# Two PSUM banks as tiles of their own, y's transposes in one earlier list, unused rows filled by DMA, and sums moved within the step

## The chip, the core and the metric

The kernel runs on one core of a Trainium2 chip. The core has a matrix engine (TensorE, PE in the profile, whose weight loads stand apart as PEld), VectorE (DVE), ScalarE (ACT), GpSimd (POOL) and SyncE (SP), which here issues every DMA. Each engine works through its own list of instructions in order and waits on semaphores for the others. The metric is the device time of one execution in microseconds (us), lower is better.

## The reference

`x` has 8 sequences of 4160 rows and 192 columns. First a causal convolution over 7 rows, with one softmax-normalised set of taps for each of 8 heads of 24 columns. Its output, 33280 rows of 192, goes through a small network: 192 to 1024, a SoLU (the hidden value times its softmax), a layer norm with a gain, and 1024 back to 192. Everything is float32.

```python
def _attn_ref(x, weight):
    w = np.exp(weight - weight.max(-1, keepdims=True))
    w = w / (w.sum(-1, keepdims=True) + 1e-09)
    x_pad = np.concatenate([np.zeros((B, K - 1, D)), x], axis=1)
    out = np.einsum('hk,bskhg->bshg', w, x_unf)     # x_unf: 7 shifted views of x_pad
...
def _moe_ref(x, w_in, w_out, g_ln):
    h = x @ w_in
    e = np.exp(h - h.max(-1, keepdims=True))
    solu = h * (e / (e.sum(-1, keepdims=True) + 1e-09))
    mu, var = solu.mean(-1, keepdims=True), solu.var(-1, keepdims=True)
    return ((solu - mu) / np.sqrt(var + 1e-06) * g_ln) @ w_out
```

## The kernel before

**Tiles, chunks, steps.** The 33280 rows are 260 tiles of 128 rows. The convolution works on chunks: chunks 0 to 2 (class `Chunk`, 8, 8 and 16 tiles) and chunks 3 to 16 (class `Strips`, 16 tiles, the last two 18). A chunk's convolution is done while the chunk before it goes through the network. From tile 8 on the network runs in steps of three tiles a, b, c (`three_steps`). As 16 is not a multiple of 3, a chunk's first tile is the first, second or third tile of a step in turn: chunk 3 first, 4 second, 5 third, and so on; chunk 2 third, 15 and 16 first.

**One tile's way.** PE multiplies y (float16 in a high and a low part) with w_in (`emit_rows` L799, `emit_third` L822) into a pair of PSUM banks. There are three pairs, for a, b and c of each step. DVE takes the maximum (`emit_max` L853), ACT the exponential (`emit_exp` L860), DVE the product (`emit_mul` L870), which is the last reader of the pair. ACT writes its high half (`emit_hi` L878), POOL the low one (`emit_lo` L890), a DMA transposes both (L892, on SP's list), and five tiles later PE multiplies them with w_out (`emit_out` L922) into a single PSUM bank. DVE evacuates it (`emit_evac` L932); POOL scales the rows (L1001); SP stores them (L1014).

**The single banks.** Of PSUM's eight banks six are the pairs. The last two are one tile, `both`, of 1024 columns. `single()` gives its halves in turn: one to each output product, and both to each group of a strip convolution. A group (`Strips.product` L385, `nc.tensor.matmul` L399) covers two heads, half of the chunk's tiles in each bank. One copy over both banks on ACT (`upper` L280) gives the high part of y in `y16`, one on DVE (`lower` L289) the low part. Heads 4 and 5 straddle a block of y16, so this group is copied in two pieces: five copies a chunk on each engine.

**y's transposes.** `y16` has three blocks of 128 columns: block 0 the high part of columns 0 to 127, block 2 their low part, block 1 both parts of the rest. Each is transposed by DMA (`turn` L419) into `yT`, in two halves of the chunk's tiles: six transposes a chunk. One copy (`double` L427) then brings part of yT's block 1 into `y2`, for the low products of L822. y16 is single, yT and y2 are double.

**The order.** `chores` says at which of its chunk's tiles k a piece of work for later chunks is due; a step takes those of its three tiles. A step's transposes are appended to the list `moves` at its end. `move()` takes one of them after each tile's p transpose: after a's, after b's, and at the end. The copy `double` is issued in the next step, after b. A step begins with the loads (`load` L356); two loads of the chunk after the next two are due at k = 13 and 14, the others at k = 1 and 3. Where a sequence begins within a chunk, POOL clears 16 rows behind the load (L365). The sums over a chunk's rows (`sum_squares` L377, DVE, "peak" in `chores`) scale y; they are due at k = 1, 4, 7 and 10 (6, 7, 9 and 10 in chunk 2, whose loads are due at k = 4 and 6) and stand near the step's end, between the maximum and the product of c. In a strip tile the partitions 48 to 63 and 112 to 127 hold nothing; `clear` (L442) sets the whole tile to zero once, on POOL, four times in all.

## Time and profile before

| | |
|---|---|
| time, median of 3 runs | 1426.57 us (1426.14 to 1429.6) |
| the profiled execution's time | 1433.29 us |
| its span, first to last instruction | 1431.6 us |
| busy: PE, DVE, ACT, POOL | 1175.8, 987.7, 950.3, 768.6 us |
| DMA queue's share of 16 engines' span | 91.8% |
| granted TensorE clock, mean | 0.935 |

The profile is of one execution. The rows below name an instruction by engine and line (PE ... L922 is line 922), with what it writes and reads (`both<-ohl,pT`). SPq is SP's list of DMA issues; the time of such a row is that of the issue, not of the transfer. Times in a timeline count from the span's start. "[0.76 <-DVE raw L932]" says that the engine was idle for 0.76 us before the row, and which instruction ended the wait.

### The profile page before, as it was taken

The numbers are of one execution on the slowest core, as the hardware profiler recorded it, in microseconds if no ns is written. First come the engines' busy times: TensorE is split into PE (matmuls) and PEld (weight loads), VectorE is DVE, ScalarE is ACT, GpSimd is POOL, SyncE is SP. The second block draws the span as 40 slices with busy tenths as digits, with TensorE's granted clock in tenths as the row PEclk, the third lists the DMA queues.
The fourth block names the chain that finished last, engine by engine and source line by source line (L and its number), as shares of the span: only waits on it lengthen the run. The fifth ranks groups of instructions, "written<-read, shape, count | busy, mean of one in ns | idle before, by whom it ended". The sixth has DMA issues, their size and how long they took to land.

```text
span 1431.6 us, 23903 instructions
## 1 busy us (share of the span) xinstructions
PE 1175.8 (82%) x8854; PEld 667.4 (47%) x8854; DVE 987.7 (69%) x1666; ACT 950.3 (66%) x1543; POOL 768.6 (54%) x751
## 2 busy tenths in 40 slices
PE   5877786979779698896969979598896969989997
PEld 3654443545445354453535545354453535545555
DVE  7755585768658586684857768377684847867777
ACT  6854565767647576584757757477674847777785
POOL 2635453646545455563654745357355536656674
PEclk8989898999989899898989989799898989999999
DMA  7696799999889989988999898799989899988977
GB/s 205 120 153 115 127 185 160 161 182 166 152 151 181 178 151 164 187 156 153 181 170 167 160 185 156 145 169 171 169 164 174 160 177 160 177 153 152 193 146 159
DMA packets 733747, 233.91 MB, mean 163 GB/s; under 512 B 649102, under 2 KB 732222, under 8 KB 733630
## 3 DMA queue, kind: packets, MB, share of 16 engines
q1 hardware_dynamic: 733630, 232.38, 91.8%
q8 instruction: 69, 1.13, 0.3%
q14 instruction: 48, 0.39, 0.1%
HBM read 40.50 MB, written 25.56 MB: 46 GB/s over the span
## 4 chain that ended last, share of the span: by engine, by line
PE 33%; DVE 19%; POOL 15%; issue 12%; ACT 8%; DMA 8%; SPq 4%; DVEq 0%; POOLq 0%; ACTq 0%
PE both L922 15%; PE ph L799 13%; POOL p L890 10%; DVE ph L853 8%; DVE e L870 7%; ACT e L860 4%; DMA xs<-in_x_dram 3%; ACT y L280 3%; PE both L399 3%; SPq L892 3%; DMA yT<-y 2%; DVE raw L932 2%; POOL raw L1001 2%; DMA pT<-p 2%; PE ph L822 1%
## 5 line engine op out<-in xcount | busy, mean ns | idle before, releaser
L890 POOL TENSOR_TENSOR p<-e,p 128x1024 f16<-128x1024 f32 x257 | 547.1, 2137 | 523.3 <-ACT p L878 523.1
L922 PE MATMUL both<-ohl,pT 128*128 128x192 f16 (+1 forms) x4264 | 568.4, 288 | 103.2 <-DVE raw L932 71.0
L922 PEld LDWEIGHTS <-pT 128*128 128x128 f16 x4264 | 394.6, 100 | 291.5 <-issue 136.5
L799 PE MATMUL ph<-whi,yT 128*128 128x512 f16 x1548 | 433.4, 390 | 78.5 <-DMA yT<-y 74.6
L860 ACT ACTIVATE e<-ph,sm 128x1024 f32<-128x1024 f32 x260 | 289.6, 1114 | 233.9 <-DVE ph L853 218.7
L853 DVE TENSOR_SCALAR_CACHE_REDUCE ph<-ph,cv 128x1024 f32<-128x1024 f32 x259 | 329.5, 1288 | 135.0 <-PE ph L799 100.1
L870 DVE SCALAR_TENSOR_TENSOR e<-ph,cv,e 128x1024 f32<-128x1024 f32 x259 | 331.0, 1278 | 28.3 <-ACT e L860 22.1
L799 PEld LDWEIGHTS <-yT 128*128 128x128 f16 x2064 | 194.7, 100 | 322.2 <-DMA yT<-y 79.0
L878 ACT CAST p<-e 128x1024 f16<-128x1024 f32 x257 | 267.0, 1039 | 83.0 <-DVE e L870 81.7
L882 ACT ACTIVATE sq<-e 128x1024 f32<-128x1024 f32 x260 | 273.4, 1051 | 0.2
L289 DVE SCALAR_TENSOR_TENSOR y<-both,s,y 128x768 f16<-128x768 f32 (+10 forms) x85 | 66.8, 805 | 212.8 <-ACT y L280 175.9
L799 PE MATMUL ph<-wlo,yT 128*128 128x512 f16 x516 | 156.3, 385 | 0.0
L932 DVE TENSOR_REDUCE raw<-both 128x192 f32<-128x384 f32 x247 | 136.7, 554 | 26.9 <-PE both L922 20.4
L280 ACT ACTIVATE y<-both,s 128x768 f16<-128x768 f32 (+10 forms) x85 | 60.1, 731 | 134.7 <-PE both L399 112.0
L822 PE MATMUL ph<-wlo,y 64*128 64x512 f16 x251 | 71.6, 390 | 49.8 <-DMA y<-yT 49.8
L1001 POOL TENSOR_SCALAR raw<-raw,t 128x192 f32<-128x192 f32 x240 | 99.8, 429 | 0.0
L822 PE MATMUL ph<-wlo,yT 64*128 64x512 f16 x269 | 75.4, 386 | 0.0
L993 POOL TENSOR_TENSOR t<-t,mhalf 128x8 f32<-128x8 f32 (+2 forms) x33 | 53.6, 1623 | 2.6
L377 DVE TENSOR_REDUCE xa<-xr 128x1 f32<-128x1536 f32 (+1 forms) x28 | 49.5, 1771 | 3.4 <-DMA xr<-in_x_dram 3.4
L860 ACT ACTIVATION_READ_ACCUMULATOR e<-ph,sm 128x1 f32 x260 | 50.1, 193 | 0.0
L377 DVE TENSOR_REDUCE xa<-xs 128x1 f32<-128x1536 f32 (+1 forms) x28 | 49.4, 1771 | 0.0
L882 ACT ACTIVATION_READ_ACCUMULATOR sq<-e 128x1 f32 x260 | 49.2, 189 | 0.0
(143 smaller groups left out, 452.9 us busy)
## 6 DMA issues: line engine op xcount, KB each, us to landing
out_dram<-raw SPq DMA_DIRECT2D x127, 192.0 KB, 2.9
xs<-in_x_dram SPq DMA_DIRECT2D x24, 576.0 KB, 7.7
xr<-in_x_dram SPq DMA_DIRECT2D x24, 576.0 KB, 7.9
pT<-p SPq DMA_TRANSPOSE x263, 4.5
y<-yT SPq DMA_DIRECT2D x12, 256.0 KB, 3.7
xr<-in_x_dram SPq DMA_DIRECT2D x6, 480.0 KB, 5.9
xs<-in_x_dram SPq DMA_DIRECT2D x4, 648.0 KB, 8.0
xr<-in_x_dram SPq DMA_DIRECT2D x4, 648.0 KB, 8.3
```

The costliest lines, as they stand in the source:

```text
L280: act.activation(self.at(0, col + e, col + z, a, b), pc[:, :, e:z], AF.Copy, scale=self.scale(),)
L799: nc.tensor.matmul(bank, lhs, w[:, r, n * 512 : (n + 1) * 512], start=start and j == 0, stop=stop and j == len(ops) - 1,)
L822: nc.tensor.matmul(banks_of(t)[n], y[q, t.off : t.off + P], wlo[q, 1, n * 512 : (n + 1) * 512], start=start, stop=not start,)
L853: dve.tensor_scalar(t.ph, t.ph, t.cv[:, 0:1], None, ALU.mult, ALU.min, accum_out=t.bias)
L860: act.activation(t.e, t.ph, AF.Exp, bias=t.bias, scale=-1.0, accum_out=grp.z[:, g : g + 1])
L870: dve.scalar_tensor_tensor(t.e, t.ph, t.cv[:, 3:4], t.e, ALU.mult, ALU.mult, accum_out=t.grp.s1[:, t.g : t.g + 1],)
L878: act.copy(t.p16[:, :, 0, :], t.halves)
L882: act.activation(junk, t.e, AF.Square, accum_out=t.grp.s2[:, t.g : t.g + 1])
L890: eng.tensor_tensor(t.p16[:, :, 1, :], t.halves, t.p16[:, :, 0, :], ALU.subtract)
L922: nc.tensor.matmul(t.po[:, 0:n], t.pT[:, a, :], w, start=j == 0, stop=j == len(ops) - 1)
L932: dve.tensor_reduce(t.grp.raw[:, t.g, :], t.po[:, 0 : 2 * D].rearrange("p (a d) -> p d a", a=2), AX.X, ALU.add,)
L1001: pool.tensor_scalar(o, o, u, 1.0, ALU.mult, ALU.mult)
```

## The change

- The two single banks become tiles of their own, `single0` and `single1`. A strip convolution takes one of each, and `upper` and `lower` copy each by itself: ten copies a chunk on each engine instead of five.
- `double` becomes an entry of the list of transposes (block 3). The list's due tiles go from 5, 5, 10, 10, 10, 10 (and 8 for the copy) to 4, 4, 7, 9, 9, 12, 12, one later in chunk 2. Chunk 2's own last transposes are all due at its first tile.
- The unused rows are filled by two DMAs from a tile of zeros, in place of a memset of the whole strip tile; the four calls move.
- From tile 16 on the sums stand at the beginning of the step's DVE work, ahead of `lower` and a's maximum.

```diff
@@ -90,14 +90,12 @@
         return ps.tile([P, F], F32, name=name, tag=f"pair{slot}")
 
     singles = 0
-    both = ps.tile([P, F], F32, name="both")
 
     def single(name):
 
         nonlocal singles
         singles += 1
-        k = singles % 2 * 512
-        return both[:, k : k + 512]
+        return ps.tile([P, 512], F32, name=name, tag=f"single{singles % 2}")
 
 
     def total(parts, name, bank=None):
@@ -384,12 +382,13 @@
 
         def product(self, h, n, a, z, bank=None):
 
-            single(f"pc_{self.ch}_{h}a"), single(f"pc_{self.ch}_{h}b")
-            self.bank = both[:, 512:F]
             m = self.nt // 2
-            pc = both[:, 512 - m * n * HD : 512 + m * n * HD].rearrange(
-                "p (t e) -> p t e", e=n * HD
-            )
+            banks = [single(f"pc_{self.ch}_{h}_{late}") for late in range(2)]
+            self.bank = banks[1]
+            pc = [
+                t[:, 0 : m * n * HD].rearrange("p (t e) -> p t e", e=n * HD)
+                for t in banks
+            ]
             for j in range(n):
                 for half, c in STRIPS:
                     late, own = (half + c) % 2, slice(64 * half, 64 * half + ROWS)
@@ -397,10 +396,7 @@
                         "p (t g) d -> p g t d", g=2
                     )
                     nc.tensor.matmul(
-                        pc[
-                            Q * c : Q * (c + 1), late * m : (late + 1) * m,
-                            j * HD : (j + 1) * HD,
-                        ],
+                        pc[late][Q * c : Q * (c + 1), :, j * HD : (j + 1) * HD],
                         taps[own, h + j, 64 * half : 64 * half + Q],
                         raw[:, c // 2, :, (h + j) * HD : (h + j + 1) * HD],
                         start=j == 0, stop=j == n - 1,
@@ -410,12 +406,24 @@
         def scale(self):
             return self.s
 
+        def upper(self, pc, h, n, a, b):
+            m = self.nt // 2
+            for late in range(2):
+                super().upper(pc[late], h, n, late * m, (late + 1) * m)
+
+        def lower(self, pc, h, n, a, b):
+            m = self.nt // 2
+            for late in range(2):
+                super().lower(pc[late], h, n, late * m, (late + 1) * m)
+
         def at(self, low, col, z, a, b):
 
             blk, c = divmod(col + low * (2 * P if col < P else R), P)
             return y16[:, blk, a:b, c : c + z - col]
 
         def turn(self, blk, a, z):
+            if blk == NB:
+                return self.double(a, z)
             nc.sync.dma_start_transpose(
                 self.yT[:, blk, a * P : z * P].rearrange("p (w t) -> p w t", t=P),
                 y16[:, blk, a:z, :].rearrange("p w d -> p (w d)"),
@@ -438,8 +446,12 @@
             )
 
     def clear(k, late):
-        a, z = (0, NTM)
-        pool.memset(strips[k][late][:, a:z, :], 0.0)
+
+        for half in range(2):
+            nc.sync.dma_start(
+                strips[k][late][64 * half + ROWS : 64 * (half + 1)],
+                zero.unsqueeze(1).broadcast_to([64 - ROWS, NTM, D]),
+            )
 
     chunks = [(Chunk if ch < OLD else Strips)(ch) for ch in range(NCH)]
 
@@ -476,6 +488,8 @@
     rebias = cp.tile([P, 1], F32, name="rebias")
     pool.memset(rebias, -916.0 * 2.0**23)
     act.activation(rebias[0:1], rebias[0:1], AF.Copy)
+    zero = cp.tile([64 - ROWS, D], F32, name="zero")
+    pool.memset(zero, 0.0)
     mhalf = cp.tile([P, 1], F32, name="mhalf")
     pool.memset(mhalf, -0.5)
     band = cp.tile([TJ, H, TB, K], F32, name="band")
@@ -1078,19 +1092,18 @@
         else:
             late = ch == 2
             if late:
-                turn(c0, c0.parts[1], 0.01, 0.2)
-                fixed("clear", (1, 4), ((1, 0), (1, 1)))
+                turn(c0, c0.parts[1], 0.001, 0.002)
+                fixed("clear", (1,), ((1, 1),))
             if c1:
                 m = c1.nt // 2
                 fixed("conv", [q + late for q in (0, 3, 6, 9)], [(c1, hg) for hg in c1.groups()])
                 fixed("open", [4], [c1])
-                fixed("turn", [5 + late] * 2 + [10 + late] * 4, [
+                fixed("turn", [q + late for q in (4, 4, 7, 9, 9, 12, 12)], [
                     (c1, q) for q in (
-                        (1, 0, m), (1, m, 2 * m), (0, 0, m), (2, 0, m),
+                        (1, 0, m), (1, m, 2 * m), (3, 0, 2 * m), (0, 0, m), (2, 0, m),
                         (0, m, 2 * m), (2, m, 2 * m),
                     )
                 ])
-                fixed("double", [8 + late], [(c1, (0, 2 * m))])
             if c2:
                 fixed("load", (4, 4, 6, 6) if late else (-1, -1, 1, 3), [(c2, j) for j in range(4)])
                 fixed("peak", (6, 7, 9, 10) if late else (1, 4, 7, 10),
@@ -1101,6 +1114,7 @@
             sums(c2, 0.75, 1.0)
             put(0.5, 0.875, "load", [(c3, j) for j in range(4)])
         if ch == 1:
+            fixed("clear", (3,), ((1, 0),))
             fixed("peak", (0, 1, 3, 4), [(c2, h) for j in range(4) for h in c2.halves(j)])
         return got
 
@@ -1254,7 +1268,6 @@
             emit_lo(q, pool)
         out_root()
         first_strips()
-        clear(0, 0)
 
     def third_two(i):
 
@@ -1287,6 +1300,7 @@
         for q in (tiles[3], t):
             emit_square(q)
         early.clear()
+        clear(0, 0)
         clear(0, 1)
         for q in (t, u):
             work = chores(q.ch, q.k, q.n)
@@ -1448,7 +1462,8 @@
                     sum_up(k, h, i - 1)
         if not start:
             root_squares()
-        if not start:
+            for k, h in work.get("peak", []):
+                sum_up(k, h, i + 2)
             lowers(0)
             emit_max(a)
         else:
@@ -1515,8 +1530,9 @@
             emit_evac(d)
         lowers(3)
         run_rows(i)
-        for k, h in work.get("peak", []):
-            sum_up(k, h, i + 2)
+        if start:
+            for k, h in work.get("peak", []):
+                sum_up(k, h, i + 2)
         run_rows(i)
         numerators(c)
         if at(3):
```

## The prediction, made before the changed kernel was run

> **What bounds the kernel now.** I read the page first (busy shares, queues), then the list of waits, then the timeline of one ordinary step, then the ends of three chunks, then the forms of the copies.

> ```profile
> span 1431.6 us, 23903 instructions
> ...
> PE 1175.8 (82%) x8854; PEld 667.4 (47%) x8854; DVE 987.7 (69%) x1666; ACT 950.3 (66%) x1543; POOL 768.6 (54%) x751
> ...
> q1 hardware_dynamic: 733630, 232.38, 91.8%
> ```

> No engine is full; PE is the busiest, and the DMA engines show 91.8%. So the list of waits (who, for whom: us in total, times, longest) says what PE lacks:

> ```profile
> PE ph L799 <- DMA yT<-y: 74.6, 9, 11.5
> PE both L922 <- DVE raw L932: 71.0, 121, 1.1
> POOL xs L365 <- DMA xs<-in_x_dram: 70.6, 6, 14.3
> ...
> PE ph L822 <- DMA y<-yT: 49.8, 4, 14.2
> ```

> Two things hold PE. Thirteen long waits for y's transposes and y's copy, 124.4 us, one at the end of nearly each chunk from chunk 2 to 14. And 121 short waits, 71.0 us, of an output product for an evacuation. Both are what the change touches. The second is read from an ordinary step that holds a convolution (timeline; start, length, [idle before it, and for what]):

> ```profile
> 776.18 0.55 DVE L932 TENSOR_REDUCE raw<-both 128x192 f32<-128x384 f32 x1
> ...
> 776.79 2.12 PE L922 MATMUL both<-ohl,pT 128*128 128x384 f16 x16 [0.76 <-DVE raw L932]
> ...
> 781.55 0.90 ACT L280 ACTIVATE y<-both,s 128x768 f16<-128x768 f32 x1 [0.88 <-PE both L399]
> ...
> 782.49 1.02 DVE L289 SCALAR_TENSOR_TENSOR y<-both,s,y 128x768 f16<-128x768 f32 x1 [2.42 <-ACT y L280]
> ...
> 787.31 0.55 DVE L932 TENSOR_REDUCE raw<-both 128x192 f32<-128x384 f32 x1
> ...
> 787.91 2.12 PE L922 MATMUL both<-ohl,pT 128*128 128x384 f16 x16 [0.20 <-DVE raw L932]
> ...
> 790.18 0.55 DVE L932 TENSOR_REDUCE raw<-both 128x192 f32<-128x384 f32 x1
> 790.42 1.11 ACT L860 ACTIVATE e<-ph,sm 128x1024 f32<-128x1024 f32 x1
> 790.65 1.74 DVE L377 TENSOR_REDUCE xa<-xs 128x1 f32<-128x1536 f32 x1
> ...
> 790.79 2.12 PE L922 MATMUL both<-ohl,pT 128*128 128x384 f16 x16 [0.76 <-DVE raw L932]
> ...
> 792.31 1.28 DVE L870 SCALAR_TENSOR_TENSOR e<-ph,cv,e 128x1024 f32<-128x1024 f32 x1
> ```

> The step repeats after 14.00 us (776.79 to 790.79). Each time the output product starts 0.05 us after the evacuation of the product just before it (790.73, 790.79), and that one lies in the other bank: singles alternate, and its own bank's last reader ended at 787.86. So PE waits for a bank that it will not write. That closes a loop: product, rows, convolution on PE, `upper` on ACT, `lower` and the two maxima on DVE, evacuation, next product.

> **The change part by part.**

> *Banks as tiles.* The wait on the other bank has no reason left; 0.96 us of the step above (0.76 and 0.20), 71.0 us in all. What is late next? PE alone needs 14.00 - 0.96 = 13.0 us. DVE: from `lower` at 782.49 to the last evacuation's end at 790.73; exp(c) ends at 791.53, so the product (L870, 1.28, quoted at 792.31 behind the sum) runs from 791.6 to 792.9, evacuation 0.55, sum 1.74, and `lower` again at 795.1: 12.6 us. So DVE comes within half a microsecond of PE, and what it loses anywhere shows. Bounds: 0 (the wait stays) and 71; I take 60, nearer the row, as DVE gives some back.

> *Copies apart.* Rows by form:

> ```profile
> L289 DVE SCALAR_TENSOR_TENSOR y<-both,s,y 128x768 f16<-128x768 f32 x36 | 36.6, 1018 | 147.6 <-ACT y L280 117.0 <-DMA yT<-y 27.7 <-DMA xs<-in_x_dram 3.0
> ...
> L280 ACT ACTIVATE y<-both,s 128x768 f16<-128x768 f32 x36 | 32.4, 901 | 93.0 <-PE both L399 81.7 <-DMA yT<-y 9.7 <-DMA xs<-in_x_dram 1.5
> ...
> L289 DVE SCALAR_TENSOR_TENSOR y<-both,s,y 128x256 f16<-128x256 f32 x12 | 5.7, 474 | 0.0
> L280 ACT ACTIVATE y<-both,s 128x256 f16<-128x256 f32 x12 | 5.6, 467 | 0.0
> ```

> A straight line through both sizes gives 250 ns fixed on ACT and 202 on DVE. 14 chunks x 5 copies become twice as many: 70 x 0.25 = 17 us of ACT, 70 x 0.20 = 14 us of DVE. The first `lower` can start after the first half of `upper`, so the pair's latency hardly moves (0.58 + 0.58 + 0.61 against 0.90 + 1.02). DVE's step goes from 12.6 to 12.8, still under PE's 13.0: no price of its own, but part of the 11 us held back above; with DVE as the bound it is the whole 14. [...]

> *y's transposes.* One transposition leaves the list after each tile's p transposition. A chunk starts on the first, second or third tile of a step (types A, B, C; chunk 3 is A, 4 B, 5 C and so on; 2 is C). I followed both lists through the three types: 0a is block 0 of the first half, 2a block 2, both needed by the next chunk's first tile.
> - Type B: the copy of y into y2 moves from behind the second tile of the step with k = 11 to 13, to the end of the step with k = 5 to 7.
> - Type C: 2a moves from behind k = 13 to behind k = 11, ahead of the next chunk's loads.
> - Type A, and chunk 2: 2a stays behind k = 12 (13 in chunk 2), behind the loads. Nothing gained.
> Block 2's second half goes out one tile later in A and B.

> ```profile
> 817.70 9.75 SPq L892 DMA_TRANSPOSE pT<-p  x1
> 827.55 2.16 SPq L419 DMA_TRANSPOSE yT<-y  x1
> ...
> 817.76 2.12 PE L922 MATMUL both<-ohl,pT 128*128 128x384 f16 x16 [0.78 <-DVE raw L932]
> ...
> 831.67 1.89 PE L799 MATMUL ph<-whi,yT 128*128 128x512 f16 x4 [7.53 <-DMA yT<-y]
> 833.35 3.82 PE L922 MATMUL both<-ohl,pT 128*128 128x384 f16 x16
> ```

> Type A: SP is stuck 9.75 us issuing one p transposition behind two loads, then issues 2a; PE goes on as it lands. Kept: 4 x 7.5 = 30, and chunk 2's 11.5. With tiles 0.3 us shorter PE comes 1 us sooner each time: +5.

> ```profile
> 647.99 1.26 SPq L419 DMA_TRANSPOSE yT<-y  x1
> ...
> 653.19 0.58 SPq L427 DMA_DIRECT2D y<-yT  x1
> ...
> 656.94 0.61 PE L822 MATMUL ph<-wlo,y 64*128 64x512 f16 x1 [10.48 <-DMA y<-yT]
> ...
> 740.37 0.25 POOL L365 MEMSET xs<- 16x192 f32 x1 [11.01 <-DMA xs<-in_x_dram]
> ...
> 745.41 1.84 SPq L419 DMA_TRANSPOSE yT<-y  x1
> ...
> 749.11 1.89 PE L799 MATMUL ph<-whi,yT 128*128 128x512 f16 x4 [9.89 <-DMA yT<-y]
> ```

> Type B (656.94): the four waits for y, 49.8, go. Next is 2a, issued at 647.99, which lands (at 4.1 us as above, 827.55 to 831.67, or somewhat less) about when PE wants it, near 651.5. In the two B chunks whose load makes POOL wait (a memset behind the load, the row at 740.37) it is 4 us late each: 8. The sum at the next chunk's start waits for a load that was issued one step before: 1.5 each, 6. Gain 36.
> Type C (749.11): 74.6 - 41.5 = 33. 2a then lands before the loads; late next is p's own transposition, which the loads and POOL's wait hold by about 3 us each: keep 12. Gain 21.
> Slow matmuls after a long wait: 3.82 against 2.12 and 1.89 against four in 1.03 us elsewhere, 2.5 us per wait. Eight waits shrink; I take 12 of 20, since remainders of 3 or 4 us may still bring it on. [...]

> *Sums.* They move to where DVE idles before `lower` (2.42 us, the sum is 1.74): free in an ordinary step. Not in chunk 2:

> ```profile
> 159.83 0.56 DVE L932 TENSOR_REDUCE raw<-both 128x192 f32<-128x384 f32 x1 [0.75 <-PE both L922]
> 166.60 1.14 DVE L289 SCALAR_TENSOR_TENSOR y<-both,s,y 128x512 f16<-128x512 f32 x2 [6.21 <-DMA yT<-y]
> ...
> 167.49 5.14 SPq L356 DMA_DIRECT2D xr<-in_x_dram  x4
> ...
> 179.22 1.75 DVE L377 TENSOR_REDUCE xa<-xr 128x1 f32<-128x1536 f32 x1 [3.36 <-DMA xr<-in_x_dram]
> ```

> In the step of tile 20 the loads are issued at its start, and the sum now stands before `lower` and the maximum. Two transpositions less before them bring the loads 3 us forward, to a landing near 176; the sum ends near 178, `lower` near 179 instead of 167.7. Behind it on DVE wait the maxima, and PE for the bank that `lower` reads: +11, from 0 (if PE makes it up at the next wait) to 13.

> *Unused rows by DMA.* POOL loses four memsets; it is 54% busy and waits for ACT: 0. SP gains eight issues of 0.58 (as at 653.19), four ahead of chunk 3's loads, whose landing releases POOL: +2.5; from 0 to 5.

> *Pressure.* With shorter steps p's transpositions behind the loads at k = 1 and 3 have about a microsecond too little: 14 chunks, +14. y16's block 2 is read one tile later in A and B: `lower` may wait, nine times, +8. Both from 0 to twice that.

> **Sum:** -60 - 36 - 21 - 12 + 5 + 11 + 2.5 + 22 = -88.5. The profiled execution (span 1431.6, time 1433.29) is 0.5% over the runs' median 1426.57; so 1345 for it, and 1338 for a run.

> **Rivals.**
> - *DMA becomes the bound.* The stretches show how full it is:

> ```profile
> 200.00:320.00 120.00, 95.29 (x725) 52.73 (x724) 80.42 (x134) 76.52 (x122) 61.02 (x61) 0.93 0.99 169
> 320.00:1260.00 940.00, 780.46 (x6015) 433.54 (x6012) 652.47 (x1058) 621.69 (x990) 509.16 (x501) 0.93 0.95 167
> ```
> If 1.00 is full, 940 us can shed only 5%: 47 us, and the time is 1380. Against it: packets' times stretch and overlap when they mix, so the share overstates the work. 0.20.
> - *The banks' wait stays*, if something else orders the products: 1338 + 60 = 1398. The start 0.05 us behind the wrong evacuation speaks against it. [...] 0.08.
> - *Slower: the sum holds DVE at each chunk's start.* It needs both loads of a half; POOL waits for the same kind of load 70.6 / 6 = 11.8 us. 13 starts x 11.8 = 153: 1338 + 153 = 1491. It decides from 88.5 / 13 = 6.8 us on. Against: the loads go out a step before. 0.09.
> - *Better: type A's waits go as well and DVE gives nothing back:* 30 + 5 + 11 more, 1292. Against: 2a of type A does not move. 0.10.

> **How the numbers follow.** The forecast itself has 0.50, by its own bounds 1305 to 1370; 0.03 for no change. The range 1290 to 1400 takes in the DMA rival, the kept wait and the better case, and leaves out the slower one and the tails. Faster by over 0.3% (what a measurement of this kernel can tell): 0.50 + 0.20 + 0.08 + 0.10 = 0.88; within: 0.03; slower: 0.09.

> **What would show it.** Right: L922's wait for L932 nearly gone; the four waits for y gone; waits for yT left at the ends of chunks 2, 3, 6, 9, 12 and near 40 us; DVE waiting some 15 us for xr near tile 20; ordinary steps near 13.0 us. Wrong: steps still at 14.0, DVE's sums waiting for loads at each chunk, or SP's issues of p's transpositions stretching everywhere (DMA full).

## The result, and the profile after

| | before | after |
|---|---|---|
| time, median | 1427.93 us (1426.14 to 1429.6, 4 runs) | 1354.55 us (1350.9 to 1359.63, 4 runs) |
| the profiled execution's span | 1431.6 us | 1352.3 us |
| granted TensorE clock, mean | 0.935 | 0.941 |

The changed kernel takes 0.9489 of the time of before, 95% interval 0.9455 to 0.9523: 73 us less. The prediction was 1338, range 1290 to 1400. In the changed kernel the line numbers are shifted: the output product is L936, its evacuation L946, `upper` L278, `lower` L287, the first product L813 and L836, the loads L354, POOL's clearing behind a load L363, the sums L375, the p transposition L906, y's transposes L427.

From the page of the changed kernel:

```profile
PE 1160.2 (86%) x8854; PEld 667.0 (49%) x8854; DVE 998.4 (74%) x1736; ACT 961.4 (71%) x1613; POOL 756.3 (56%) x748
...
q1 hardware_dynamic: 736062, 234.15, 100.2%
```

PE does the same 8854 matmuls in 15.6 us less (1175.8 before); the other 64 us of the span are idle time of PE that went. The list of waits of the changed kernel:

```profile
POOL xs L363 <- DMA xs<-in_x_dram: 89.7, 6, 23.6
...
DVE xa L375 <- DMA xr<-in_x_dram: 71.4, 11, 17.3
PE po L936 <- DVE y L287: 68.7, 14, 16.3
PE ph L813 <- DMA yT<-y: 66.7, 11, 12.3
...
DVE xa L375 <- DMA xs<-in_x_dram: 55.7, 10, 10.6
...
PE po L936 <- DMA pT<-p: 19.8, 5, 16.9
...
PE po L936 <- DVE raw L946: 3.3, 5, 1.0
```

The output product's 121 waits for an evacuation (71.0 us) are 5 (3.3 us). The four waits for y (49.8 us) have no row any more. New are the third row, PE waiting for `lower` (19.3 us before), and the two rows of DVE, whose sums wait 127.1 us for loads; before, DVE's sums waited 3.4. An ordinary step with a convolution (timeline):

```profile
662.29 2.12 PE L936 MATMUL po<-ohl,pT 128*128 128x384 f16 x16
...
671.03 0.55 DVE L946 TENSOR_REDUCE raw<-po 128x192 f32<-128x384 f32 x1
...
671.50 1.74 DVE L375 TENSOR_REDUCE xa<-xr 128x1 f32<-128x1536 f32 x1
...
673.35 1.14 DVE L287 SCALAR_TENSOR_TENSOR y<-pc,s,y 128x384 f16<-128x384 f32 x2
...
675.09 2.12 PE L936 MATMUL po<-ohl,pT 128*128 128x384 f16 x16
```

The step is 12.80 us long (662.29 to 675.09) where it was 14.00, and the product has no wait. The sum lies between the evacuation and `lower`, where DVE waited 2.42 us for `upper` in the step before the change. The same sum at a chunk's start (the first step of chunk 9, timeline):

```profile
706.70 2.15 SPq L354 DMA_DIRECT2D xs<-in_x_dram  x2
...
709.39 1.05 ACT L278 ACTIVATE y<-pc,s 128x384 f16<-128x384 f32 x2 [0.52 <-PE pc L398]
...
714.86 0.25 POOL L363 MEMSET xs<- 16x192 f32 x1 [15.75 <-DMA xs<-in_x_dram]
...
715.89 2.11 POOL L904 TENSOR_TENSOR p<-e,p 128x1024 f16<-128x1024 f32 x1
...
718.91 1.75 DVE L375 TENSOR_REDUCE xa<-xs 128x1 f32<-128x1536 f32 x1 [10.64 <-DMA xs<-in_x_dram]
...
720.58 1.13 DVE L287 SCALAR_TENSOR_TENSOR y<-pc,s,y 128x384 f16<-128x384 f32 x2
...
721.24 4.00 PE L936 MATMUL po<-ohl,pT 128*128 128x384 f16 x16 [9.30 <-DVE y L287]
```

`upper` is done at 710.4, but `lower` stands behind the sum, the sum behind a load issued at 707, and PE behind `lower`, whose bank it is to write: 9.30 us. POOL stands behind the same load with its clearing of 16 rows, and the low part of p behind that.

### The profile page after: what moved, and what is told of

Its sections match the earlier page's. It is cut to its first block, busy times and chain, and to the rows that moved or that the text cites. A ratio compares the mean times of both kernels' runs of the same rounds, so it can differ in the third digit from the quotient of the medians.

```text
span 1352.3 us, 24085 instructions
## 1 busy us (share of the span) xinstructions
PE 1160.2 (86%) x8854; PEld 667.0 (49%) x8854; DVE 998.4 (74%) x1736; ACT 961.4 (71%) x1613; POOL 756.3 (56%) x748
## 3 DMA queue, kind: packets, MB, share of 16 engines
q1 hardware_dynamic: 736062, 234.15, 100.2%
## 4 chain that ended last, share of the span: by engine, by line
PE 26%; POOL 19%; issue 17%; DMA 16%; DVE 10%; ACT 7%; SPq 6%; POOLq 0%; DVEq 0%; ACTq 0%
POOL p L904 13%; PE po L936 12%; PE ph L813 11%; DMA xr<-in_x_dram 5%; DMA xs<-in_x_dram 5%; SPq L906 4%; DVE e L884 3%; DVE ph L867 2%; POOL raw L1015 2%; ACT e L874 2%; DMA pT<-p 2%; POOL t L1007 2%; ACT p L892 2%; DMA yT<-y 2%; ACT sq L896 2%
## 5 line engine op out<-in xcount | busy, mean ns | idle before, releaser
L904 POOL TENSOR_TENSOR p<-e,p 128x1024 f16<-128x1024 f32 x257 | 546.8, 2136 | 441.3 <-ACT p L892 416.2
L936 PE MATMUL po<-ohl,pT 128*128 128x192 f16 (+1 forms) x4264 | 565.3, 291 | 92.2 <-DVE y L287 68.7
L936 PEld LDWEIGHTS <-pT 128*128 128x128 f16 x4264 | 396.3, 100 | 268.2 <-issue 98.2
L813 PE MATMUL ph<-whi,yT 128*128 128x512 f16 x1548 | 428.4, 386 | 69.4 <-DMA yT<-y 66.7
L813 PEld LDWEIGHTS <-yT 128*128 128x128 f16 x2064 | 193.7, 99 | 309.3 <-DMA yT<-y 72.1
L892 ACT CAST p<-e 128x1024 f16<-128x1024 f32 x257 | 267.1, 1040 | 44.5 <-DVE e L884 35.4
L813 PE MATMUL ph<-wlo,yT 128*128 128x512 f16 x516 | 154.0, 380 | 0.0
L946 DVE TENSOR_REDUCE raw<-po 128x192 f32<-128x384 f32 x247 | 136.7, 553 | 18.9 <-PE po L936 18.8
L287 DVE SCALAR_TENSOR_TENSOR y<-pc,s,y 128x384 f16<-128x384 f32 (+7 forms) x158 | 77.7, 535 | 60.3 <-ACT y L278 47.7
L278 ACT ACTIVATE y<-pc,s 128x384 f16<-128x384 f32 (+7 forms) x158 | 72.3, 518 | 64.7 <-PE pc L398 46.6
L375 DVE TENSOR_REDUCE xa<-xr 128x1 f32<-128x1536 f32 (+1 forms) x28 | 49.6, 1775 | 71.4 <-DMA xr<-in_x_dram 71.4
L375 DVE TENSOR_REDUCE xa<-xs 128x1 f32<-128x1536 f32 (+1 forms) x28 | 49.5, 1775 | 57.7 <-DMA xs<-in_x_dram 55.7
L836 PE MATMUL ph<-wlo,yT 64*128 64x512 f16 x269 | 74.1, 380 | 0.2 <-DMA yT<-y 0.2
L836 PE MATMUL ph<-wlo,y 64*128 64x512 f16 x251 | 68.7, 380 | 0.0
L363 POOL MEMSET xs<- 16x192 f32 x7 | 1.7, 248 | 100.2 <-DMA xs<-in_x_dram 89.7
```

Of the source, the lines that this page charges most:

```text
L375: dve.tensor_reduce(self.part[:, col : col + 1], self.raw[j][:, a:z, :], AX.XY, ALU.max, apply_absolute_value=True,)
L813: nc.tensor.matmul(bank, lhs, w[:, r, n * 512 : (n + 1) * 512], start=start and j == 0, stop=stop and j == len(ops) - 1,)
L836: nc.tensor.matmul(banks_of(t)[n], y[q, t.off : t.off + P], wlo[q, 1, n * 512 : (n + 1) * 512], start=start, stop=not start,)
L892: act.copy(t.p16[:, :, 0, :], t.halves)
L904: eng.tensor_tensor(t.p16[:, :, 1, :], t.halves, t.p16[:, :, 0, :], ALU.subtract)
L936: nc.tensor.matmul(t.po[:, 0:n], t.pT[:, a, :], w, start=j == 0, stop=j == len(ops) - 1)
```

## The experiments

Times of different groups are compared by their ratio to the kernel before, timed on the same chip in the same group; 0.01 is 14.3 us. In the groups of these runs the kernel before took 1429 to 1431 us.

**Only the banks, only the list, only the sums.** Three kernels, each the kernel before with one part of the change.

```diff
 e1: -    both = ps.tile([P, F], F32, name="both")
     +    return ps.tile([P, 512], F32, name=name, tag=f"single{singles % 2}")
     ...  (and product, upper, lower as in the change)
 e2: -    fixed("turn", [5 + late] * 2 + [10 + late] * 4, ...   -  fixed("double", [8 + late], ...
     +    fixed("turn", [q + late for q in (4, 4, 7, 9, 9, 12, 12)], ...
 e3: +    for k, h in work.get("peak", []):      (ahead of lowers(0) and a's maximum)
     +        sum_up(k, h, i + 2)
```

> The kernel before, with one edit: the two single banks are tiles of their own, copied apart. My theory (the 71 us for which PE waited on the other bank's evacuation were a wait on the whole tile, and PE is the bound between the long waits): 1365 us, 55 to 70 less than before; the waits of L922's products for the evacuation nearly gone, ordinary steps near 13.0 instead of 14.0 us, the 124 us of long waits unchanged or a little longer. Rival one (the DMA queue is the bound, with a floor near 1350): the short waits go, but the long ones grow by as much, and the time stays above 1400. Rival two (something else orders the products): no change, 1428.

Measured 1371.05 us, 0.9578 (0.9548 to 0.9607): 60 us less, the prediction's term. Its waits:

```profile
PE ph L805 <- DMA yT<-y: 87.0, 11, 12.6
...
PE ph L828 <- DMA y<-yT: 57.5, 5, 17.1
...
PE po L928 <- DMA pT<-p: 13.3, 7, 6.9
PE pc L398 <- DVE raw L938: 13.2, 16, 5.0
...
PE po L928 <- DVE y L287: 5.0, 3, 3.3
...
PE po L928 <- DVE raw L938: 3.3, 3, 2.1
```

The banks' 71.0 us are 3.3. PE's wait for `lower` fell as well, 19.3 to 5.0, and the convolution's wait for an evacuation rose from 4.4 to 13.2. Most of what came back is on the DMA side: 144.5 us of long waits where 124.4 were, and 13.3 for pT where 7.7 were. The steps are shorter, the transposes no faster where the pages give it: in the changed kernel, which has the same banks, a p transposition took 4.7 us in the median from issue to landing, 4.5 before. The run holds the split tiles and the separate copies together; the two were not tried singly.

> The kernel before, with one edit: y's transposes and copy in one list with the earlier due tiles, and chunk 2's own last transposes at its first tile. My theory: the four waits for y's copy (49.8 us) and the waits at the ends of chunks 5, 8, 11 (28 us) shrink, those at 2, 3, 6, 9, 12 stay; 1428 - 55 = 1373 us, between 1360 and 1385. Rival (DMA bound): the waits move to p's transposes, and the time stays above 1410.

Measured 1376.52 us, 0.962 (0.9591 to 0.9649): 55 us less. Its waits:

```profile
PE both L924 <- DVE raw L934: 68.4, 116, 1.1
...
PE ph L801 <- DMA yT<-y: 46.4, 9, 11.5
...
PE both L924 <- DVE y L289: 39.7, 10, 9.1
...
PE both L924 <- DMA pT<-p: 15.2, 7, 4.9
```

The waits for y are gone and those for yT 28 us shorter. Back come 20 us of waits for `lower`, and 7.5 for pT.

> The kernel before, with one edit: the sums stand ahead of `lower` and a's maximum from tile 16 on. My theory (free in an ordinary step, but at a chunk's start DVE is held until both loads of the first half have landed): slower, 1440 to 1470 us; DVE waits 80 to 130 us for xr and xs, and PE waits for DVE's `lower` some 40 us. Rival (the sums' move is what made the changed kernel faster): 1390 or less.

Measured 1440.95 us, 1.0063 (1.0043 to 1.0084): slower by 9 us, 0.6%. Its sums wait 47.7 and 33.0 us for loads, and PE waits 34.6 us for `lower`, 17.4 of it in the step of tile 20.

Together the first three give -60 - 55 + 9 = -106 us, where the change gave -73. Where the rest went is what the next runs ask.

**The first sum late.** The changed kernel, with each chunk's first sum back at the step's end.

```diff
+                if h[1]:
                     sum_up(k, h, i + 2)
```

> The changed kernel, with one edit: the first sum of each chunk, the one that waits for loads, goes back to the step's end; the other three stay early. My theory: PE's 68.7 us of waits for `lower` go nearly all, 1354 - 50 = 1304 us, between 1290 and 1325. Rival (DMA bound, its queue at 100% of the changed kernel's span): the waits turn into waits for p's and y's transposes, and the time stays at 1340 or more.

Measured 1349.71 us, 0.9436 (0.9408 to 0.9463). I had expected much more from this one sum. PE's waits for `lower` fell from 68.7 to 27.4 us, but those for pT rose from 19.8 to 37.8 us, and DVE's second to fourth sums still wait (20.0 and 16.8 us). The rival that named a full DMA queue had the time right, so the queue was tried itself, and beside it two other things that stand behind loads. All four kernels that follow rest on this one.

```diff
 e5: -    out[...].rearrange("(g p) d -> p g d", p=P), self.raw[:, a:z, :]
     +    out[...].rearrange("(g p) d -> p g d", p=P)[0:64], self.raw[0:64, a:z, :]
 e6:      move()                                 # end of the step
     +    if any(q[0:2] == (0, 0) for k, q in work.get("turn", []) ...):
     +        move()
 e7: -    pool.memset(t[64 * half : 64 * half + HALO, w, :], 0.0)    # behind the load
     +    halos.append(lambda q=q: pool.memset(q, 0.0))              # run behind emit_lo(b)
 e8: e6 and e7
```

> The changed kernel with each chunk's first sum back at the step's end (as in the run before), and of every output store only the first 64 of its 128 rows: the same number of issues on SP, half of their bytes, so some 13 MB of 234 MB less on the DMA queue; half of the output is not written. Theory 1 (the DMA engines' throughput is what ate some 35 us of the two parts' separate gains): the waits for transposes and loads shrink all over, and the time falls by about the share of the bytes, 5%, to 1290 (1275 to 1315). Rival (order on SP's list, one transposition behind a load, and POOL's wait for its load, not throughput): the few long waits stay, and the time is 1335 to 1350.

Measured 1340.0 us, 0.9373 (0.9353 to 0.9393). Half of the output is not written, so this kernel serves for its time alone. With 221.62 MB instead of 234.15 on the queue, 5.4% less, the time fell by 9 us, 0.7%. The time that the packets took fell by less than the bytes, from 100.5% of 1349.0 us to 98.7% of 1337.8, which is 35 us or 2.6%. Had it been the limit, the time would have fallen by about as much and not by 9 us. Only the stores were made smaller; the same with fewer transposes was not tried.

> As before with the first sum at the step's end, and at the end of the step whose list takes up block 0 and block 2 of the first half, both go out at once, ahead of the next step's loads. Theory (the long waits for yT at the chunks' ends, 64.8 us, come from block 2 standing behind loads): these waits fall below 20 us, L813's row for yT nearly goes; time 1300 to 1320, if nothing else is late. Rival 1 (the DMA queue is full): the waits move to pT or to the next chunk's loads and the time stays at 1340 to 1355. Rival 2: the second transposition at the step's end delays c's p transposition or the next one, and PE's waits for pT grow from 38 to over 60 us, time unchanged.

Measured 1345.29 us, 0.9411 (0.9389 to 0.9433). L813's wait for yT fell from 64.8 to 1.4 us, as expected, but the time by only 4 us, no more than the two intervals leave open. Two rows took its place:

```profile
PE po L936 <- DMA pT<-p: 55.9, 25, 6.8
...
PE po L936 <- DVE y L287: 41.3, 16, 7.6
```

They had 37.8 and 27.4; and a single wait of 17.8 us for DVE's product is new. So the long waits for yT covered waits that were ready behind them. Where the waits went, and the time, are what the first rival said; that a full queue is the reason is not shown by it.

> As before with the first sum at the step's end, and POOL's clearing of 16 rows behind a load is put behind the low part of b, some 9 us later in the step, instead of right behind the load's issue. POOL waits 100.3 us for it in 7 places, and a's low part, its transposition and the output products five tiles on stand behind it. Theory (POOL's wait is a good part of what is lost): POOL's wait for xs falls below 30 us, PE's waits for pT (37.8 us) fall by half, time 1315 to 1330. Rival (POOL's wait overlaps the waits for yT at the same chunk ends, or the DMA queue is the limit): POOL's wait goes and the time stays within 8 us of 1350.

Measured 1333.94 us, 0.9324 (0.9298 to 0.935): 16 us less than with the first sum late alone. POOL's wait fell from 100.3 to 28.4 us. PE's waits for pT did not halve (38.1); those for yT fell by 12. The time is 4 us above the theory's range, and 8 us below the rival's.

> The two edits of the two runs before this one together. If order on SP's list and POOL's wait are the causes, the gains add: 1275 to 1300. If the DMA queue is full: 1335 to 1350, and the queue's share of 16 engines' span above 100%. If each only uncovers the other, this one alone falls, to about 1300, while the two single edits stay near 1345.

Measured 1329.64 us, 0.9303 (0.9276 to 0.933), some 20 us less than their base, what the two gave singly (4 and 16). The gains add, as the first case had it, but they were so small that the time, 1329.64, lies in none of the three ranges. The queue's share is 101.6%.

**All sums late; clearing on POOL; loads from ACT.** The first is the changed kernel with all its sums back at the step's end and nothing else undone. The second and third rest on e8.

```diff
 e9:  -    for k, h in work.get("peak", []):  sum_up(k, h, i + 2)     (ahead of lowers(0))
 e10: +    pool.memset(strips[k][late][:, a:z, :], 0.0)               (for the two DMAs, at the old places)
 e11: -    nc.sync.dma_start(t[own], ...      +    nc.scalar.dma_start(t[own], ...
```

> The changed kernel with all four sums of a chunk back at the step's end, where the kernel before has them; the banks, the list and the clearing by DMA stay. Theory (the early sums are a price in the step in which a load is late, and nothing elsewhere): the wait of the first lower copy for the loads goes with all of them, time 1345 to 1352, the same as with the first sum alone put back. Rival (early sums take DVE's work away from the step's end and so are a part of the gain): 1358 to 1370, slower than the changed kernel's 1354.6.

Measured 1332.96 us, 0.9316 (0.9283 to 0.935). Against the changed kernel's 0.9489 that is 0.0173, 25 us: the sums early cost that much, and my expectation, that the first sum was the whole price, was wrong. Its waits:

```profile
PE ph L813 <- DMA yT<-y: 62.9, 10, 12.2
...
PE po L936 <- DVE y L287: 14.4, 4, 6.4
```

PE's wait for `lower` falls from 68.7 us to 14.4. The waits for yT stay as in the changed kernel.

> The run with the first sum late, two transpositions at the step's end and POOL's clearing of halo rows later, and in it the unused rows are cleared as in the kernel before: four memsets of whole strip tiles on POOL at their old places, no clearing by DMA. Theory (the clearing DMAs stand with chunk 3's loads ahead of a p transposition, and PE waits 15.9 us for it at 88.9 us; before, this place cost 5.4): that wait falls to about 5, time 10 us less, 1317 to 1322. Rival (the loads of chunk 3 alone make the wait, or the clearing on POOL delays p's low parts by as much): no difference, 1327 to 1335.

Measured 1319.59 us, 0.9225 (0.919 to 0.9259): 11 us less than with the clearing by DMA. The place is the start of chunk 3's loads. First the timeline of its base e8, which clears by DMA, then this kernel's:

```profile
64.99 4.30 SPq L459 DMA_DIRECT2D xs<-zero  x2
...
69.34 5.49 SPq L361 DMA_DIRECT2D xs<-in_x_dram  x3
...
74.94 11.86 SPq L914 DMA_TRANSPOSE pT<-p  x1
...
88.88 3.38 PE L944 MATMUL po<-ohl,pT 128*128 128x192 f16 x20 [15.94 <-DMA pT<-p]
```

```profile
59.23 2.98 POOL L458 MEMSET xs<- 128x3456 f32 x1
...
65.53 2.28 SPq L361 DMA_DIRECT2D xs<-in_x_dram  x3
...
67.92 13.38 SPq L910 DMA_TRANSPOSE pT<-p  x1
...
83.36 4.02 PE L940 MATMUL po<-ohl,pT 128*128 128x192 f16 x24 [8.09 <-DMA pT<-p]
```

Four clearing DMAs stand ahead of chunk 3's loads; the two shown, the last of them, hold SP for 4.30 us. POOL's memset took 2.98 us, and POOL is busy for 58% of this kernel's span. The loads go out 3.8 us sooner and the p transposition 7.0 us sooner, and PE's wait is 8.09 us in place of 15.94.

> The same base as the run before (clearing by DMA), and the strip tiles' loads are issued from ACT's list instead of SP's. Theory (what is left of PE's waits for pT, 63 us, comes from p's transpositions that stand behind a load in SP's order): SP's issues of pT fall to some 2 us each, PE's waits for pT fall below 30 us, time 1300 to 1315. Rival 1 (the transposition is slow because the DMA engines are busy with the load, wherever it was issued): issues or landings stay long, time 1325 to 1335. Rival 2 (ACT is held by issuing, 0.6 to 5 us a load, and the copies and exponentials behind it are late): slower, 1335 to 1380.

Measured 1378.7 us, 0.9652 (0.96 to 0.9703): 50 us slower than its base. The p transposition's row in e8 and here (how many, then the duration of the issue in ns, least, median and most):

```profile
L914 SPq DMA_TRANSPOSE pT<-p x257: 1568/2308/11864, 39.1 to 1312.4; - x129
```

```profile
L914 SPq DMA_TRANSPOSE pT<-p x257: 1560/2282/12461, 39.5 to 1353.2; - x129
```

With the loads on another engine's list and queue the longest issue of a p transposition is as long as before. In e8 48 of the 257 issues began while a load was still on its way, and here 47: these took 5.9 us on average in e8 and 5.7 here, the others 2.4 and 2.5. So SP's order alone did not hold the transposition: it was as long beside a load issued from another list. Nor did it come through sooner: from issue to landing it took 16.9 us at most against 13.4 in e8.

The time is just within the second rival's range, 1335 to 1380. ACT's issue of a load takes 0.32 us mostly, so ACT is not held by the issuing itself. But it is held by the load's wait:

```profile
295.00 8.66 ACTq L361 DMA_DIRECT2D xr<-in_x_dram  x2
303.71 1.06 ACT L904 ACTIVATE sq<-e 128x1024 f32<-128x1024 f32 x1 [7.67 <-DMA xr<-in_x_dram]
```

The second of these two loads went out 0.02 us after a p transposition had landed, and ACT stood still until then (idle 7.67 us before L904). By the trace 15 of the 56 loads went out so, right behind the landing of a transposition of p or y, and ACT was idle ahead of them for some 50 us in all; its idle time before L904 alone is 33.6 us, where e8 has 0.2. PE's idle time is 31 us longer, in several rows. How much of the 50 us comes from ACT's standing still was not tried.

**The combination.** e10 with all sums late, so e9, e6, e7 and e10 in one.

> The run with clearing on POOL, two transpositions at the step's end and the halo rows' clearing later, and in it all four sums of a chunk at the step's end, not the first alone. Theory (prices add where they stand at different places: all sums late against only the first late was worth 0.0120 of the time of the kernel before, 17 us): 1298 to 1308, and PE's waits for the lower copies (43.1 us) fall below 20. Rival (the other edits have taken this wait's cover already, so that the second to fourth sum find room before the lower copy): 1315 to 1322.

Measured 1312.06 us, 0.918 (0.9162 to 0.9197, five rounds), between what theory and rival gave: late sums are worth 6 us here, give or take 5, where they were worth 17 beyond the first one with the other edits absent. PE's waits for the lower copies fell from 43.1 to 29.3 us, not below 20. It is the fastest of all, 117 us under before and 44 us (0.9489 to 0.918) under the changed kernel. A line of its page, and two of its waits:

```profile
q1 hardware_dynamic: 733630, 232.38, 103.1%
```
```profile
PE po L940 <- DMA pT<-p: 55.4, 25, 7.7
...
PE po L940 <- DVE y L287: 29.3, 10, 6.8
```

## Why the prediction was right, and where its sum was off

| step | predicted, us | measured, us | from |
|---|---|---|---|
| banks as tiles | -60 | -60 | e1 |
| the list (B -36, C -21, slow matmuls -12, A +5) | -64 | -55 | e2 |
| sums early | +11 | +25 (+9 by e3) | changed kernel against e9 |
| clearing by DMA | +2.5 | +11 | e10 against e8 |
| pressure | +22 | +6, what is left | -73 less the four above |
| sum | -88.5 | -73 | |

The first two terms are uncertain by about 4 us each, the sums and the clearing, as differences of two ratios, by 6 to 7, and so the last line of terms by some 12. Besides, the terms were measured on different bases: banks and list on the kernel before, the sums on the changed kernel, the clearing on e8.

Faster was right, and so were the two large terms, banks and list, within 9 us, with the waits that they name gone. The time alone would not decide it: 1354.55 lies between the forecast's 1338 and the DMA rival's 1380. By the table, the 15 us between forecast and result are the list (9 us less gained) and the prices of sums and clearing (22 us more), less 16 us that the pressure did not cost. But how sums and pressure share their cost depends on where the sums are measured. Added to the kernel before (e3) they cost 9 us, as forecast, and 22 us are left for the pressure, as forecast too; taken out of the changed kernel they cost 25, and 6 are left. What the runs show is that the sums cost more once the other parts are in, which the prediction had in neither term.

**Banks.** The wait on the bank that PE does not write was the cause; it went with the tiles apart, and the step is 12.80 us where 13.0 was forecast. The 11 us held back were right in size but not in kind: on DVE's side PE lost 9 us at the convolution and won 14 at `lower`, and it was the transposes that took 26 us back in e1. So that the term came out as it did, with other gains and losses than those it was made of, is in part luck.

**The list, chunk by chunk.** The prediction kept 46.5 us of waits for yT at the ends of chunks 2, 3, 6, 9 and 12 and 8 us at the ends of the type B chunks. The trace shows the end of chunk 6, one of the first kind, so:

```profile
559.31 1.89 PE L813 MATMUL ph<-whi,yT 128*128 128x512 f16 x4 [10.44 <-DMA yT<-y]
```

The five ends hold 12.3, 8.8, 10.4, 7.0 and 10.7 us, 49.2 in all; the ends of chunks 4, 7, 10 and 13 hold 16.0, twice the 8 forecast. Type C lost its wait for yT as forecast. What took its place is not the p transposition (12 us forecast) but the early sum, at the starts of chunks 6, 9 and 12: 10.1, 9.3 and 7.7 us, the rows at 721.24 above being the second. With the sums late (e9) the same three places do wait for pT, 4.3, 7.6 and 4.9 us: 16.8. So "late next" was named rightly for the transposes alone, and the step failed by leaving the sum out of type C.

**Sums.** At tile 20 a delay of 11 us was forecast; PE's wait there is 16.32, where it was 2.88 before, and DVE waits 17.27 us for the load before it can begin the sum:

```profile
170.25 1.75 DVE L375 TENSOR_REDUCE xa<-xr 128x1 f32<-128x1536 f32 x1 [17.27 <-DMA xr<-in_x_dram]
...
172.79 3.97 PE L936 MATMUL po<-ohl,pT 128*128 128x384 f16 x16 [16.32 <-DVE y L287]
```

For type B 1.5 us each were set; starts 5, 8, 11 and 14 wait 2.1, 4.6, 3.4 and 7.4. The slower rival was this very mechanism, the sum holding DVE at a chunk's start, at 11.8 us for 13 starts. It is real at seven of them and at tile 20, at 2 to 16 us, so its price is 9 to 25 us, by e3 or e9, and not 153. Behind the other chunks' ends it has no row: there PE waits for yT first.

**Clearing.** For the eight issues I took the price of a small DMA, 0.58 us. In the changed kernel six of them took 0.60 to 1.11 us, but the last two ahead of chunk 3's loads 1.92 and 2.49, and they stand at the one place where the p transposition waits for the loads behind them.

**The DMA rival.** The queue's share is 100.2% in the changed kernel, and 103.1% in the fastest one, in 1306.5 us. The share was no ceiling here, as the prediction argued. The same 733630 packets and 232.38 MB took 91.8% of 1431.6 us before, 1314 us, and 103.1% of 1306.5 us in the fastest kernel, 1347 us: the same packets' own time was 33 us longer in a span 125 us shorter, so the share overstates the work. That it is their mixing that stretches them was not shown by itself. And with 5.4% fewer bytes the time fell by 0.7%. But something on the side of the DMA is what is left: most of the waits of PE that grew as others went are for transposes, or for `lower`, which stands behind transposes and loads (e6 against e4: 37.8 to 55.9 us for pT, 27.4 to 41.3 for `lower`).

**Slow matmuls.** 12 us were taken; PE's busy time fell by 15.6 us with the same number of matmuls, at a mean granted clock of 0.941 in place of 0.935. What part of it belongs to which wait was not tried, so this term is not shown by itself.

## What to carry to other kernels

If a wait ends on an instruction that uses another part of the same tile, split the tile; here that was worth 60 us, with the copies apart that go with it, found by two rows 0.05 us apart. An early place for a piece of work was free only in steps where its own input had long landed (no wait of the output product in the ordinary step, 9.30 us at the start of chunk 9): look at the step in which the input is latest, and at what stands behind the work on its engine. And when several long waits end at the same place, taking the longest away shows the next (e6: 63 us of waits gone, 4 us of time won), so price each by what is late after it.

## What the runs showed of the hardware that I had not expected

The DMA queue's share of 16 engines' span passed 100% and was no ceiling here: it was 100.2% in the changed kernel and 103.1% in the fastest one, 44 us shorter. The issue of a p transposition, 1.6 us at the least, took up to 13.4 us behind loads on the same list (e10), and 12.5 us when the loads came from another engine's queue (e11), so another queue was no way around a load here.

PE's clock fell after a shorter wait than the 3 or 4 us that I had reckoned with (two rows of the changed kernel's timeline, and four of its stretches: length, then PE's busy time first, and the granted clock as the third number from the end):

```profile
408.07 3.41 PE L936 MATMUL po<-ohl,pT 128*128 128x384 f16 x16 [2.06 <-DVE y L287]
...
888.39 2.12 PE L936 MATMUL po<-ohl,pT 128*128 128x384 f16 x16 [3.36 <-DVE y L287]
```
```profile
405.31:408.72 3.41, 1.34 (x10) 0.58 (x8) 2.83 (x5) 0.54 (x2) 0.00 (x0) 1.00 1.16 263
408.72:412.13 3.41, 3.41 (x15) 1.97 (x14) 3.28 (x7) 1.74 (x3) 0.00 (x0) 0.50 1.12 208
...
883.26:886.67 3.41, 1.78 (x8) 0.59 (x6) 0.83 (x1) 1.62 (x4) 1.92 (x2) 1.00 1.30 128
886.67:890.08 3.41, 1.69 (x14) 1.27 (x15) 2.95 (x6) 0.00 (x0) 0.00 (x0) 1.00 1.13 244
```
